# Second-stage weights split once, half of them kept and half reloaded; ScalarE shares the counting in every routing phase

## The chip, the cores and the metric

One core of one Trainium2 chip runs the whole program. The metric is the device time of an execution in microseconds (us). The core's engines work side by side, each through its own fixed list of instructions in order: TensorE (PE, matrix products, with its weight loads shown as PEld), VectorE (DVE), ScalarE (ACT), GpSimd (POOL), and SyncE (SP), which here only issues transfers (DMAs). An engine that has to wait for another stands still, and everything behind the waiting instruction in its list stands with it.

## The reference

```
x = attention(q, k, v, M_prev, z_prev, beta)      # 4 batches x 576 tokens = 2304 tokens, 512 wide
logits = x @ w_gate                               # 8 experts
order = argsort(-logits.flatten())                # greedy: best pair of token and expert first
# a token is given to the first expert in that order that has fewer than cap = 288 tokens
for e in range(8):
    h = maximum(x[mask_e] @ w1[e], 0)             # 512 -> 1024
    out[mask_e] = h @ w2[e]                       # 1024 -> 512
# second layer, the same for all tokens
h = out @ w_in                                    # 512 -> 2048, float64 in the inputs
g = h * clip(h + 3, 0, 6) / 6
return g @ w_out                                  # 2048 -> 512, float64 in the inputs
```

Results are wanted at float32 precision, so the kernel writes each float32 operand of a product as the sum of a rounded part (hi) and what is left (lo), and makes three products: hi hi, hi lo, lo hi.

## The kernel before

**Two stages.** First comes the attention with the gate's logits. While it runs, class `Convert` turns w_in and w_out from float64 into float32, 28 of 32 pieces (`PRE`), and stores them in a DRAM tensor `wb`. Then comes `experts`: eight turns of one loop, numbered s = 0 to 7 here and below. Turn s takes the 288 tokens of the expert that fills up as number s, through that expert's own weights (kind 0, 8 blocks f of 128 hidden units) and then through the shared second layer (kind 1, 16 blocks f). A step of the loop is one block: `l1` (12 products of 128x128 by 288 columns into `h`), an activation that leaves `gh` and `gl`, and two steps later (`LAG`) `l2` (12 products into four accumulators).

**The weights.** The shared layer's weights lie in one float32 tile `WB`, 16 blocks of 128x1024. `split_w` makes hi and lo of each half block afresh for every step of all eight turns: ScalarE copies the 512 columns to `wh`, and GpSimd subtracts to get `wl`, with every sixth subtraction on VectorE (`EVERY`). `ahead` runs this up to three steps (`SPLIT`) before the products. An expert's own weights come by DMA into `raw` (four buffers) and are split in the same way. The last 4 of the 32 float64 pieces are converted in the first two steps of turn 0 (`rest`), into `WB`; the other 28 are loaded from `wb` in seven transfers of 1 MB.

**The routing.** `Router.phase(s)` finds which expert fills up as number s and with which tokens. It is a chain, run on VectorE for the most part, cut into units by `yield`; `step()` works them into turn s - 1 at a fixed rate per step (`RATE`). From phase 2 on, keys go out to DRAM and come back spread over all partitions (`kd<-ks`, `rHw<-kd`, `rLw<-kd`, issued by SP). Two searches follow (`search`), of four rounds each. A round compares all 2304 16-bit values with a threshold T per partition and counts them (L714), turns the counts round (L723) and picks the next T (L726), so a round starts from the result of the one before. In phase 0 alone, which runs at the end of the attention, ScalarE counts 864 of the values with a Sign (L717), and one small instruction (L718) adds its count. The routing for s = 7 is trivial, so turns 6 and 7 have no search, and turn 5 has only the end of a phase.

**What sets the order.** The code's order gives the dependences; a scheduler then fixes each engine's list at build time. On SP too, a transfer whose buffer is not yet free holds up those behind it.

Of the kernel before, what the change touches and what calls it, by code (L numbers as in the profile page):

```python
# [28 lines left out]
SHARE = 432  # L29
# [485 lines left out]
class Router:  # L515
# [188 lines left out]

    def search(self, W, need, row, shared):


        nc, wk = self.nc, self.wk
        T = self.T0
        W, cmp = [x.rearrange("p b s -> p (b s)") for x in (W, self.cmp)]  # L710
        n = W.shape[1] - shared
        for s in range(4):
            cnt = wk.tile([128, 1], F32, name="cnt", bufs=2)
            nc.vector.tensor_scalar(cmp[:, :n], W[:, :n], T, 0.0, op0=OP.is_ge, op1=OP.add, accum_out=cnt)  # L714
            if shared:
                below = wk.tile([128, 1], F32, name="below", bufs=2)
                nc.scalar.activation(cmp[:, n:].bitcast(BF), W[:, n:], AF.Sign, bias=T, scale=-1.0, accum_out=below)  # L717
                nc.vector.scalar_tensor_tensor(cnt, below, -0.5, cnt, op0=OP.mult, op1=OP.add)  # L718
            if s == 0:
                yield 0  # L720
            else:
                nc.vector.tensor_scalar(self.G[:, s, 32:], T, self.cz[:, s:s + 1], None, op0=OP.add)
            nc.vector.transpose(row[:, s, :32], cnt.to_broadcast([128, 32]))  # L723
            fl = wk.tile([128, 33], F32, name="fl", bufs=2)
            T = wk.tile([128, 1], F32, name="T", bufs=4)
            nc.vector.scalar_tensor_tensor(fl, row[:, s], need, self.G[:, s], op0=OP.is_ge, op1=OP.mult, accum_out=T)  # L726
            yield SLACK
        self.found = T
# [76 lines left out]
    def phase(self, s):  # L805
# [6 lines left out]
        if s < E - 1:  # L812
# [10 lines left out]
            else:  # L823
                self.by_dram()
                yield BACK
            half = SHARE if s == 0 else 0
            Hs = self.search(self.Hw, cap - half, self.rowH, 2 * half)
# [11 lines left out]
            c = self.rowH[:, :, :32]  # L839
            if half:  # L840
                nc.vector.tensor_scalar(m, c, float(half), None, op0=OP.add)
                c = m
            nc.vector.scalar_tensor_tensor(m, c, cap, c, op0=OP.is_lt, op1=OP.mult)
# [109 lines left out]
class Convert:  # L953
# [51 lines left out]

    def rest(self, WB):

        for i in range(self.pre, len(self.src)):
            w = WB[:, i // 2, i % 2 * 512:(i % 2 + 1) * 512].rearrange("p (k n) -> p k n", k=4)
            self.load(i)  # L1010
            self.bits(w.bitcast(I32), i)
            self.sign(w, w, i)
            yield i // 2


def experts(ctx, tc, rt, x_dram, cv, w1, w2, out, ident, cap, B, S):
# [9 lines left out]
    NEXT = 12, 11  # L1026
    CONV = 2, 8
    EARLY = 6
    res = ctx.enter_context(tc.tile_pool(name="eres", bufs=1))
# [3 lines left out]
    rt.late(ctx, ps)  # L1033
    WB = res.tile([128, FB, 1024], F32, name="WB")

# [32 lines left out]

    def load_expert(s, f):
        if f == 0:  # L1070
# [5 lines left out]
        nc.sync.dma_start(raw[:, 512:], w2[bass.ds(e, 1), f * 128:(f + 1) * 128, :].rearrange("o p n -> p (o n)"))  # L1076
        raws[s, f] = raw

    W = {}
    cnt = [0]  # L1080

    def split_w(i, part):
        s, kind, f = order[i]
        src = (WB[:, f, :] if kind else raws[s, f])[:, part * 512:(part + 1) * 512]
        hi, lo = [wp.tile([128, 512], F32R, name=f"w{z}{part}", tag=f"w{z}{part}", bufs=SPLIT[part]) for z in "hl"]
        cnt[0] += 1
        nc.scalar.activation(hi, src, AF.Copy)  # L1087
        v = cnt[0] % EVERY == 0 or cnt[0] <= FIRST
        j = (nc.vector if v else nc.gpsimd).tensor_tensor(lo, src, hi.bitcast(F32), op=OP.subtract)  # L1089
        if s == 0 and kind == 0:  # L1090
            after(tc, j, rt.last if v else rt.fetch)
        W[i, part] = hi, lo
        if part and kind == 0 and f + RAW < FA:
            load_expert(s, f + RAW)

# [105 lines left out]
    def ahead(i):  # L1201

        for part, n in ((0, SPLIT[0]), (1, SPLIT[1] - LAG)):
            while nw[part] < min(i + n, len(order)):
                split_w(nw[part], part)
# [69 lines left out]
def body(ctx, tc, q, k, v, M_prev, z_prev, beta, w_gate, w1, w2, w_in, w_out, out, dbg=None):  # L1275
# [71 lines left out]
```

## Time and profile before

| | us |
|---|---|
| median of 3 runs | 1165.59 (1163.01 to 1169.36) |
| profiled execution: time / its span | 1169.76 / 1168.0 |
| attention and routing phase 0 | up to 346 |
| turns 0 to 7 of `experts` | 125.1, 112.0, 108.0, 108.8, 106.7, 93.0, 83.5, 75.0 |

A turn is counted here from the end of the turn before to the copies of its own result out of the accumulators (`yo`, L1130), read from the trace, to half a microsecond. Busy times are sums of the durations of an engine's instructions. TensorE's busy time is not its speed: successive 288-column products start 0.13 us apart at the full clock and 0.24 us apart at half of it, while each is shown some 0.3 to 0.6 us long, since they overlap. What TensorE waited for, and the clock it was granted, say more.

### The profile page before, as it was taken

The numbers are of one execution on the slowest core, as the hardware profiler recorded it, in microseconds if no ns is written. First come the engines' busy times: TensorE is split into PE (matmuls) and PEld (weight loads), VectorE is DVE, ScalarE is ACT, GpSimd is POOL, SyncE is SP. The second block draws the span as 40 slices with busy tenths as digits, with TensorE's granted clock in tenths as the row PEclk, the third lists the DMA queues.
The fourth block names the chain that finished last, engine by engine and source line by source line (L and its number), as shares of the span: only waits on it lengthen the run. The fifth ranks groups of instructions, "written<-read, shape, count | busy, mean of one in ns | idle before, by whom it ended". The sixth has DMA issues, their size and how long they took to land.

```text
span 1168.0 us, 20128 instructions
## 1 busy us (share of the span) xinstructions
PE 984.3 (84%) x6748; PEld 903.9 (77%) x6748; DVE 854.6 (73%) x1935; ACT 673.2 (58%) x1627; POOL 664.1 (57%) x514
## 2 busy tenths in 40 slices
PE   4988898897228797898899798879978999999997
PEld 3666776675128697888798788779978999999996
DVE  7788887886867987868866976897497755455453
ACT  5776876774326354445545463555545567667674
POOL 7666666461436364654565465547544567767773
PEclk9999998898559888889999898899898899999999
DMA  7888878875344023121132023104201400401100
GB/s 173 241 232 250 241 191 254 225 202 162 149 150 194 1 87 86 61 92 41 55 112 64 1 80 107 44 1 134 81 16 39 127 22 19 147 21 37 57 2 21
DMA packets 103560, 123.17 MB, mean 105 GB/s; under 512 B 19744, under 2 KB 70304, under 8 KB 102560
## 3 DMA queue, kind: packets, MB, share of 16 engines
q1 hardware_dynamic: 99120, 108.22, 32.1%
q0 software_dynamic: 3072, 9.44, 2.7%
q10 hardware_dynamic: 1264, 4.22, 0.9%
q8 instruction: 53, 0.87, 0.3%
q14 instruction: 51, 0.42, 0.1%
HBM read 85.88 MB, written 17.22 MB: 88 GB/s over the span
## 4 chain that ended last, share of the span: by engine, by line
PE 41%; DVE 35%; DMA 12%; issue 7%; ACT 3%; SPq 2%; POOL 1%; POOLq 0%; DVEq 0%; ACTq 0%
DVE rcmp L714 9%; PE acc L1099 5%; PE acc L1100 5%; PE h L1170 5%; PE h L1167 5%; PE acc L1098 5%; PE h L1168 5%; DMA rHw<-kd 3%; DVE gl L1188 3%; PE av L328 3%; PE rp L701 3%; DVE t L1186 2%; DVE wl L1089 1%; DMA raw<-in_moe_w_in_dram 1%; DVE fl L726 1%
## 5 line engine op out<-in xcount | busy, mean ns | idle before, releaser
L1089 POOL TENSOR_TENSOR wl<-WB,wh 128x512 fp32r<-128x512 f32 x215 | 290.6, 1367 | 216.9 <-ACT wh L1087 198.2
L1099 PE MATMUL acc<-gl,wh 128*128 128x288 f32 x768 | 237.8, 318 | 54.4 <-DVE gl L1188 48.2
L1100 PE MATMUL acc<-gh,wl 128*128 128x288 f32 x768 | 232.1, 311 | 0.0
L1099 PEld LDWEIGHTS acc<-gl,wh 128*128 128x128 f32 x768 | 156.1, 203 | 62.7 <-DVE gl L1188 55.6
L1098 PE MATMUL acc<-gh,wh 128*128 128x288 f32 x768 | 196.9, 312 | 8.6 <-ACT gh L1187 8.6
L1087 ACT ACTIVATE wh<-WB 128x512 fp32r<-128x512 f32 x256 | 159.3, 631 | 39.5 <-PE acc L1099 35.8
L1089 POOL TENSOR_TENSOR wl<-raw,wh 128x512 fp32r<-128x512 f32 x100 | 134.4, 1357 | 66.5 <-ACT wh L1087 61.8
L1100 PEld LDWEIGHTS acc<-gh,wl 128*128 128x128 f32 x768 | 156.2, 203 | 0.0
L1167 PE MATMUL h<-yh,wh 128*128 128x288 f32 x512 | 147.1, 308 | 1.3 <-ACT pc L1185 1.3
L1098 PEld LDWEIGHTS acc<-gh,wh 128*128 128x128 f32 x768 | 138.2, 200 | 10.5 <-ACT gh L1187 10.1
L1168 PE MATMUL h<-yh,wl 128*128 128x288 f32 x512 | 145.3, 304 | 0.0
L1188 DVE SCALAR_TENSOR_TENSOR gl<-t,gh 128x288 fp32r<-128x288 f32 x128 | 104.3, 823 | 35.9 <-ACT gh L1187 35.8
L1186 DVE SCALAR_TENSOR_TENSOR t<-t,pc 128x288 f32<-128x288 f32 x128 | 75.8, 594 | 63.4 <-ACT pc L1185 63.3
L1184 ACT ACTIVATE t<-h,rthree 128x288 f32<-128x288 f32 x128 | 63.7, 497 | 98.3 <-PE h L1170 75.6
L1187 ACT ACTIVATE gh<-t 128x288 fp32r<-128x288 f32 x128 | 56.3, 443 | 100.7 <-DVE t L1186 100.6
L1167 PEld LDWEIGHTS h<-yh,wh 128*128 128x128 f32 x512 | 101.4, 198 | 3.5 <-ACT pc L1185 2.8
L282 ACT ACTIVATE P<-P,mx 128x128 f32<-128x128 f32 (+2 forms) x144 | 83.7, 583 | 34.6 <-DVE mx L267 33.1
L1168 PEld LDWEIGHTS h<-yh,wl 128*128 128x128 f32 x512 | 101.3, 198 | 0.3 <-POOL wl L1089 0.2
L1170 PE MATMUL h<-yl,wh 128*128 128x288 f32 x512 | 96.4, 309 | 5.6 <-DVE yl L1158 5.6
L1087 ACT ACTIVATE wh<-raw 128x512 fp32r<-128x512 f32 x128 | 81.6, 640 | 21.3 <-issue 10.4
L1170 PEld LDWEIGHTS h<-yl,wh 128*128 128x128 f32 x512 | 79.6, 198 | 7.6 <-DVE yl L1158 7.0
L1181 DVE TENSOR_TENSOR gl<-t,gh 128x288 fp32r<-128x288 f32 x64 | 51.3, 801 | 38.4 <-ACT gh L1180 38.2
(283 smaller groups left out, 2360.6 us busy)
## 6 DMA issues: line engine op xcount, KB each, us to landing
raw<-in_moe_w_dram SPq DMA_DIRECT2D x128, 256.0 KB
kh<-knh SPq DMA_DIRECT2D x60, 144.0 KB
raw<-in_moe_w_in_dram SPq DMA_DIRECT2D x16, 512.0 KB
raw<-in_moe_w_out_dram SPq DMA_DIRECT2D x16, 512.0 KB
wb<-wf SPq DMA_DIRECT2D x28, 256.0 KB
kn<-in_k_dram SPq DMA_DIRECT2D x16, 288.0 KB
qn<-in_q_dram SPq DMA_DIRECT2D x16, 288.0 KB
qs<-qnh SPq DMA_DIRECT2D x30, 144.0 KB
```

What stands on the lines that cost most here:

```text
L282: nc.scalar.activation(x[:, :w], x[:, :w], AF.Exp, bias=mx, scale=-1.0, accum_out=col)
L714: nc.vector.tensor_scalar(cmp[:, :n], W[:, :n], T, 0.0, op0=OP.is_ge, op1=OP.add, accum_out=cnt)
L1087: nc.scalar.activation(hi, src, AF.Copy)
L1089: j = (nc.vector if v else nc.gpsimd).tensor_tensor(lo, src, hi.bitcast(F32), op=OP.subtract)
L1098: nc.tensor.matmul(p, ah, bh, start=first, stop=False)
L1099: nc.tensor.matmul(p, ah, bl, start=False, stop=False)
L1100: rt.behind = nc.tensor.matmul(p, al, bh, start=False, stop=last)
L1167: nc.tensor.matmul(p, wk[k][0], x[k][0], start=(k == 0), stop=False)
L1168: nc.tensor.matmul(p, wk[k][1], x[k][0], start=False, stop=False)
L1170: rt.behind = nc.tensor.matmul(p, wk[k][0], x[k][1], start=False, stop=(k == KC - 1))
L1186: nc.vector.scalar_tensor_tensor(t, t, 6.0, pc, op0=OP.min, op1=OP.mult)
L1188: nc.vector.scalar_tensor_tensor(gl, t, 1.0 / 6.0, gh.bitcast(F32), op0=OP.mult, op1=OP.subtract)
```

## The change

`split_w` now splits the shared weights only in turn 0. Odd blocks f get their hi and lo written into `WB`, which has become a tile of 8 blocks x 2 halves x (512 hi + 512 lo), as many bytes as before, and they stay there. Even blocks are split into a rotating tile `w0` or `w1`, written to a new DRAM tensor `hl` by SP, and in turns 1 to 7 read back, 16 transfers of 512 KB a turn. In turn 0 the float32 blocks come through the `raw` buffers, one transfer each; the four unconverted pieces are converted when their block's turn in `load` comes (`conv`), one per step. In turns 1 to 7 all remaining subtractions (kind 0) are GpSimd's. `ahead` runs as far as the rotating tiles allow, up to six steps. And the sharing of the count with ScalarE holds in all phases.

```diff
@@ search
-            if shared:
-                below = wk.tile([128, 1], F32, name="below", bufs=2)
-                nc.scalar.activation(cmp[:, n:].bitcast(BF), W[:, n:], AF.Sign, bias=T, scale=-1.0, accum_out=below)
-                nc.vector.scalar_tensor_tensor(cnt, below, -0.5, cnt, op0=OP.mult, op1=OP.add)
+            below = wk.tile([128, 1], F32, name="below", bufs=2)
+            nc.scalar.activation(cmp[:, n:].bitcast(BF), W[:, n:], AF.Sign, bias=T, scale=-1.0, accum_out=below)
+            nc.vector.scalar_tensor_tensor(cnt, below, -0.5, cnt, op0=OP.mult, op1=OP.add)
@@ phase
-            half = SHARE if s == 0 else 0
+            half = SHARE
-            if half:
-                nc.vector.tensor_scalar(m, c, float(half), None, op0=OP.add)
-                c = m
+            nc.vector.tensor_scalar(m, c, float(half), None, op0=OP.add)
+            c = m
@@ experts
-    WB = res.tile([128, FB, 1024], F32, name="WB")
+    WB = res.tile([128, FB // 2, 2, 1024], F32R, name="WB")
+    hl = cv.dram.tile([FB // 2, 2, 128, 1024], F32, name="hl")
+    def load(s, j):
+        if j >= FA + FB * (s == 0):
+            return
+        if j >= FA:
+            f = j - FA
+            raw = raws[s, 1, f] = wp.tile([128, 1024], F32, name="raw", tag="raw", bufs=RAW)
+            if f < cv.pre // 2:
+                nc.sync.dma_start(raw, cv.wb[:, f])
+            else:
+                conv.extend([lambda u=u: cv.rest(raw[:, u * 512:(u + 1) * 512], 2 * f + u) for u in range(2)])
+            return
...
@@ split_w
-        src = (WB[:, f, :] if kind else raws[s, f])[:, part * 512:(part + 1) * 512]
-        hi, lo = [wp.tile([128, 512], F32R, name=f"w{z}{part}", tag=f"w{z}{part}", bufs=SPLIT[part]) for z in "hl"]
+        if kind and f % 2:
+            w = WB[:, f // 2, part]
+        else:
+            w = wp.tile([128, 1024], F32R, name=f"w{part}", tag=f"w{part}", bufs=SPLIT[part])
+        hi, lo = w[:, :512], w[:, 512:]
+        W[i, part] = hi, lo
+        if kind and s:
+            if f % 2 == 0:
+                nc.sync.dma_start(w.bitcast(F32), hl[f // 2, part])
+            return
+        src = raws[s, kind, f][:, part * 512:(part + 1) * 512]
         cnt[0] += 1
         nc.scalar.activation(hi, src, AF.Copy)
-        v = cnt[0] % EVERY == 0 or cnt[0] <= FIRST
+        v = s == 0 and (cnt[0] % EVERY == 0 or cnt[0] <= FIRST)
         j = (nc.vector if v else nc.gpsimd).tensor_tensor(lo, src, hi.bitcast(F32), op=OP.subtract)
...
+        if kind and f % 2 == 0:
+            nc.sync.dma_start(hl[f // 2, part], w.bitcast(F32))
+        if part:
+            load(s, f + kind * FA + RAW)
@@ ahead
-        for part, n in ((0, SPLIT[0]), (1, SPLIT[1] - LAG)):
-            while nw[part] < min(i + n, len(order)):
+        for part in range(2):
+            while nw[part] < min(i + 2 * SPLIT[0], len(order)):
+                held = [j for j in range(i - part * LAG, nw[part] + 1) if j >= 0 and not (order[j][1] and order[j][2] % 2)]
+                if len(held) > SPLIT[part] or order[nw[part]][0] not in reg or order[nw[part]][:1] + (0, 0) not in raws:
+                    break
                 split_w(nw[part], part)
                 nw[part] += 1
@@ before and in the loop
-    for f in range(0, EARLY, 2):
-        nc.sync.dma_start(WB[:, f:f + 2], cv.wb[:, f:f + 2])
-    rest = cv.rest(WB)
+    for i in range(2):
+        cv.load(cv.pre + i)
...
-        if s == 0 and f % FA < CONV[1]:
-            for _ in range(CONV[0]):
-                next(rest, None)
+        if conv:
+            conv.pop(0)()
```

Two places show what this does to the engines' lists. The first is ScalarE's list in turn 3, at the searches of phase 4; `t`, `pc` and `gh` are the three activations of a step of kind 1, `wh0` and `wh1` the hi copies of a half block. Before:

```order
L1184 ACTIVATE t_7653<-h_7626,rthree_181 128x288
L1185 ACTIVATE pc_7654<-h_7626 128x288
L1087 ACTIVATE wh0_7660<-WB_4127 128x512
L1087 ACTIVATE wh1_7664<-WB_4127 128x512
L1187 ACTIVATE gh_7651<-t_7653 128x288
```

In the changed kernel, at the same place (`rcmp, below` is the Sign with its count, `T` the threshold that VectorE found in the round before):

```order
L1204 ACTIVATE t_7591<-h_7555,rthree_181 128x288
L1205 ACTIVATE pc_7592<-h_7555 128x288
L716 ACTIVATE rcmp_178,below_7634<-rHw_176,T_7575 128x864
L1207 ACTIVATE gh_7589<-t_7591 128x288
L716 ACTIVATE rcmp_178,below_7695<-rHw_176,T_7640 128x864
L1204 ACTIVATE t_7625<-h_7598,rthree_181 128x288
L1205 ACTIVATE pc_7626<-h_7598 128x288
```

The two copies of each step are gone, and a Sign stands in their place, sometimes ahead of the next step's `t` and sometimes behind its `pc`.

The second place is SP's list around the keys of phase 4. Before, the way out and the two ways back stand together:

```order
L1076 DMA raw_7957<-in_moe_w2_dram 128x512
L759 DMA kd_7541<-ks_7540 64x576
L762 DMA rHw_176<-kd_7541 128x1x2304
L762 DMA rLw_177<-kd_7541 128x1x2304
L1074 ISA
L1074 DMA raw_8189<-in_moe_w1_dram 128x4x128
```

In the changed kernel the reads of `hl` stand ahead of them and between them:

```order
L1102 DMA w1_7428<-hl_4128 128x1024
L1102 DMA w0_7395<-hl_4128 128x1024
L1102 DMA w0_7479<-hl_4128 128x1024
L758 DMA kd_7444<-ks_7443 64x576
L1102 DMA w1_7481<-hl_4128 128x1024
L761 DMA rHw_176<-kd_7444 128x1x2304
L761 DMA rLw_177<-kd_7444 128x1x2304
L1102 DMA w0_7551<-hl_4128 128x1024
```

One read of `hl` has moved between the way out and the first way back, and the two before the way out wait for buffers that the products of earlier steps set free.

## Rows read from the trace of the kernel before

**Rows 1.** Stretches by turn, 0 to 7: busy us (instructions), granted clock, DMA share, GB/s.

```profile
346.40:471.50 125.10, 105.68 (x661) 99.89 (x662) 101.23 (x198) 64.41 (x147) 64.04 (x48) 0.86 0.28 93
471.50:583.50 112.00, 96.25 (x654) 91.56 (x653) 91.85 (x180) 57.43 (x135) 60.84 (x46) 0.92 0.21 63
583.50:691.50 108.00, 95.27 (x636) 92.14 (x635) 82.05 (x153) 56.52 (x134) 59.34 (x46) 0.91 0.22 64
691.50:800.30 108.80, 91.27 (x635) 87.91 (x634) 85.29 (x154) 55.77 (x133) 60.01 (x46) 0.92 0.20 62
800.30:907.00 106.70, 93.38 (x633) 90.17 (x633) 80.14 (x154) 56.52 (x132) 58.76 (x46) 0.90 0.21 63
907.00:1000.00 93.00, 90.58 (x651) 89.71 (x650) 57.83 (x111) 56.00 (x130) 59.81 (x46) 0.94 0.19 59
1000.00:1083.50 83.50, 81.10 (x602) 80.22 (x601) 43.28 (x62) 56.05 (x129) 59.11 (x46) 0.98 0.21 66
1083.50:1158.50 75.00, 74.64 (x566) 74.10 (x564) 36.97 (x55) 49.44 (x112) 48.54 (x37) 1.00 0.05 16
```

The engines in each row are PE, PEld, DVE, ACT and POOL, in that order.

**Rows 2.** Page of the profile: the chain's shares by engine, and ScalarE's copies of WB.

```profile
PE 41%; DVE 35%; DMA 12%; issue 7%; ACT 3%; SPq 2%; POOL 1%; POOLq 0%; DVEq 0%; ACTq 0%
...
L1087 ACT ACTIVATE wh<-WB 128x512 fp32r<-128x512 f32 x256 | 159.3, 631 | 39.5 <-PE acc L1099 35.8
```

**Rows 3.** Waits in the whole span: total us, times, longest us.

```profile
ACT gh L1187 <- DVE t L1186: 100.6, 46, 5.0
...
PE acc L1099 <- DVE gl L1188: 48.2, 32, 4.4
...
DVE rcmp L714 <- DMA rHw<-kd: 18.9, 6, 5.0
```

**Rows 4.** VectorE by line in 691 to 800 us: busy us, mean ns, idle before.

```profile
L1188 DVE SCALAR_TENSOR_TENSOR gl<-t,gh 128x288 fp32r<-128x288 f32 x16 | 15.3, 966 | 0.4 <-ACT gh L1187 0.4
L1186 DVE SCALAR_TENSOR_TENSOR t<-t,pc 128x288 f32<-128x288 f32 x16 | 9.5, 594 | 5.9 <-ACT pc L1185 5.9
L714 DVE TENSOR_SCALAR_CACHE_REDUCE rcmp<-rLw,T 128x2304 uint16<-128x2304 uint16 x3 | 7.8, 2611 | 0.1
...
L1089 DVE TENSOR_TENSOR wl<-WB,wh 128x512 fp32r<-128x512 f32 x5 | 4.6, 924 | 0.0
...
L1089 DVE TENSOR_TENSOR wl<-raw,wh 128x512 fp32r<-128x512 f32 x3 | 2.0, 681 | 0.0
```

**Rows 5.** Tile rcmp: ns min/median/max, first and last start, forms.

```profile
L714 DVE TENSOR_SCALAR_CACHE_REDUCE rcmp<-rHw,T x21: 1711/2611/2615, 301.2 to 859.5; 128x2304 uint16<-128x2304 uint16 x18, 128x1440 uint16<-128x1440 uint16 x3
...
L717 ACT ACTIVATE rcmp<-rHw,T x3: 1014/1014/1016, 301.2 to 309.1; 128x864 bf16<-128x864 uint16 x3
L717 ACT ACTIVATION_READ_ACCUMULATOR rcmp<-rHw,T x3: 186/186/187, 302.1 to 310.0; 128x1 f32 x3
```

**Rows 6.** Line 718, the added count, in phase 0: ns min/median/max.

```profile
L718 DVE SCALAR_TENSOR_TENSOR cnt<-below,cnt x8: 142/160/1534, 298.9 to 325.5; 128x1 f32<-128x1 f32 x8
```

**Rows 7.** Line 1188 in the whole span: ns min/median/max.

```profile
L1188 DVE SCALAR_TENSOR_TENSOR gl<-t,gh x128: 414/608/2064, 399.6 to 1155.2; 128x288 fp32r<-128x288 f32 x128
```

**Rows 8.** VectorE, then GpSimd, in order of time around 748 us: start us, length us.

```profile
748.67 1.51 DVE L1188 SCALAR_TENSOR_TENSOR gl<-t,gh 128x288 fp32r<-128x288 f32 x1
...
745.71 4.16 POOL L1089 TENSOR_TENSOR wl<-WB,wh 128x512 fp32r<-128x512 f32 x3 [6.57 <-ACT wh L1087]
```

**Rows 9.** Chain that ended last, from 815 us: start us, length us, what.

```profile
840.27 6.85 DMA rHw<-kd
```

**Rows 10.** Stretch in which loads of 1 MB from wb run (columns as in rows 1).

```profile
313.00:316.00 3.00, 0.00 (x0) 0.00 (x0) 3.00 (x6) 0.00 (x0) 0.63 (x1) 0.50 1.00 410
```

**Rows 11.** GpSimd, then TensorE, in order of time from 337 us, at turn 0's start.

```profile
337.12 5.26 POOL L1064 DMA_INDIRECT xg<-x_dram,ids  x1 [23.49 <-DVE rleft L916]
...
344.55 0.92 POOL L1064 DMA_INDIRECT xg<-x_dram,ids  x1 [0.30 <-issue]
...
346.38 2.41 PE L1113 MATMUL xt<-ident,xg 96*128 96x96 f32 x12 [10.15 <-DMA xg<-x_dram,ids]
```

More of the change, by code (lines that the diff above doesn't have):

```diff
@@ L1004, in run, with rest @@
                                    f.rearrange("p k n -> p (k n)").bitcast(F32))
[L1006 to L1013, printed above, removed]
+    def rest(self, w, i):
+        w = w.rearrange("p (k n) -> p k n", k=4)
+        self.bits(w.bitcast(I32), i)
+        self.sign(w, w, i)
+        if i + 2 < len(self.src):
+            self.load(i + 2)
 def experts(ctx, tc, rt, x_dram, cv, w1, w2, out, ident, cap, B, S):
@@ L1026, in experts @@
     NEXT = 12, 11
-    CONV = 2, 8
-    EARLY = 6
     res = ctx.enter_context(tc.tile_pool(name="eres", bufs=1))
@@ L1067, in gather @@
             rt.fetch = i
-    def load_expert(s, f):
+    def load(s, j):
[9 more added lines that the diff above has]
+            return
+        f = j
         if f == 0:
@@ L1076, in load_expert @@
         nc.sync.dma_start(raw[:, 512:], w2[bass.ds(e, 1), f * 128:(f + 1) * 128, :].rearrange("o p n -> p (o n)"))
-        raws[s, f] = raw
+        raws[s, 0, f] = raw
     W = {}
+    conv = []
     cnt = [0]
@@ L1091, in split_w @@
             after(tc, j, rt.last if v else rt.fetch)
-        W[i, part] = hi, lo
-        if part and kind == 0 and f + RAW < FA:
-            load_expert(s, f + RAW)
+        if kind and f % 2 == 0:
+            nc.sync.dma_start(hl[f // 2, part], w.bitcast(F32))
+        if part:
+            load(s, f + kind * FA + RAW)
     def mm3(p, lhs, rhs, first, last):
@@ L1225, in experts @@
     for f in range(RAW):
-        load_expert(0, f)
-    for f in range(0, EARLY, 2):
-        nc.sync.dma_start(WB[:, f:f + 2], cv.wb[:, f:f + 2])
-    rest = cv.rest(WB)
+        load(0, f)
+    for i in range(2):
+        cv.load(cv.pre + i)
     cv.behind = rt.last
@@ L1232, in experts @@
         pass
-    for f in range(EARLY, cv.pre // 2, 2):
-        i = nc.scalar.dma_start(WB[:, f:f + 2], cv.wb[:, f:f + 2])
-        after(tc, i, rt.xin)
     def step():
@@ L1246, in experts @@
             for u in range(RAW):
-                load_expert(s + 1, u)
+                load(s + 1, u)
             xs = x_in(s + 1)
@@ L1293, in body @@
     cv = Convert(ctx, tc, w_in, w_out, wb, PRE)
+    cv.dram = dram
     with ExitStack() as actx:
```

## The prediction

> **What bounds the kernel now.** I read the stretches by turn first [rows 1]. Turn 7, without any routing, takes 75.0 us at a granted clock of 1.00, with TensorE busy throughout: that is what 24 steps cost TensorE. Turn 6, with the tail of a phase but no search, takes 83.5 us. Turns 1 to 4, with searches, take 106.7 to 112.0 us at a clock of 0.90 to 0.92. So some 25 us of each of these four turns come with the routing, though its products are few. What differs between the rows is VectorE: busy for 37.0 us in turn 7, 43.3 in turn 6, 57.8 in turn 5, and 80.1 to 91.9 in turns 1 to 4. Next the chain that ended last: VectorE has 35% of it, ScalarE 3%, GpSimd 1% [rows 2]. Then the waits [rows 3]: TensorE's largest is for `gl`, 48.2 us in 32 waits; ScalarE waits 100.6 us for VectorE's `t` before it can make `gh`; and VectorE itself stands 18.9 us at the first comparison of six phases, because the keys have not come back. VectorE's list is in order, so a `gl` behind a comparison waits for it. GpSimd and ScalarE are busy for little over half of a turn [rows 1], so work taken off them counts only by what it does to VectorE.
>
> **The change, part by part.** All sums are for the profiled execution, 1169.76 us. I work them out in turn 3 (85.3 us of VectorE) and carry them to the others.
>
> *Counting.* A comparison of 2304 values takes 2.61 us, one of 1440 takes 1.71 [rows 5]. Eight rounds a phase give 8 x 0.90 = 7.2 us less. Each round gains the added count, 0.160 us by its median in phase 0 [rows 6], and the phase gains one small addition to `m`, which I count as a ninth of these: 1.4 us more. ScalarE's Sign takes 1.01 + 0.19 = 1.20 us [rows 5], less than the 1.71 beside it, so it is hidden when it starts within half a microsecond of the comparison. What it costs when it does not is a rival below.
>
> *Splitting, on VectorE.* In turns 1 to 7 VectorE no longer subtracts: in turn 3 that takes away 4.6 + 2.0 = 6.6 us [rows 4].
>
> *Splitting, on GpSimd.* 32 subtractions of kind 1 a turn go, and with them a collision. In turn 3 `gl` takes 966 ns and `t` 594 on average [rows 4], while the shortest `gl` takes 414 [rows 7]. One `gl` took 1.51 us beside a row of three GpSimd subtractions of 1.39 us each [rows 8]. Without them I take 450 ns for both, near the shortest: 16 x 0.516 + 16 x 0.144 = 10.6 us. The bounds are 0 (if the lengthening is VectorE's own) and 16 x 0.552 + 16 x 0.180 = 11.7.
>
> The Trainium skill has a rule for this (SBUF — State Buffer, section "SBUF: two separate sides"): GpSimd and a VectorE instruction with two SBUF inputs share one port pair under an exclusive lock, and whichever comes second waits out the whole of the first. By that rule all of the lengthening goes where GpSimd falls silent, so the sum would stand at 10.6. It also speaks against the change in one place: in kind 0 of turns 1 to 7 GpSimd now does all 16 subtractions, so `gl` there stays long.
>
> *Splitting, on ScalarE.* 32 copies of 631 ns a turn go [rows 2], 20 us, and 8 Signs come, 9.6 us. I count nothing for it: ScalarE stood mostly waiting for VectorE [rows 3]. That gain has a bound of its own in the first rival.
>
> VectorE's 85.3 us in turn 3 so become 85.3 - 7.2 + 1.4 - 6.6 - 10.6 = 62.3. For what that is worth I go by the rows of turns 4 and 5: between 80.1 us busy (106.7 us long) and 57.8 (93.0) a microsecond of VectorE is worth 13.7 / 22.3 = 0.61 of the turn [rows 1]. This slope has the waits and the lost clock in it. With the same 23.0 us off, turn 1 becomes 99.7 us (12.3 less), turn 2 93.8 (14.2), turn 3 95.7 (13.1), turn 4 92.6 (14.1). Turn 5 has no rounds left (the last comparison of the keys starts at 859.5 us [rows 5], in turn 4), keeps the end of a phase, and loses 17 us of VectorE; it cannot fall below turn 6, and I take 86 (7 less). Turn 6 gives 1.5, turn 7 nothing. Sum: 62.2.
>
> *Turn 0.* The splits stay. The shorter rounds give 5.8 x 0.61 = 3.5. At its start TensorE waits 10.15 us for the gather, whose first list took GpSimd 5.26 us to write and its third 0.92, while VectorE was converting two pieces [rows 11]; these now come in mid-turn. The most this can give is 4.3; I take 3. Sum with the turns: 68.7.
>
> *Reloading.* 16 reads of 512 KB a turn, 8.4 MB. From `wb`, of the same form, the transfers reached 410 GB/s with every DMA engine busy [rows 10], so the reads take 20 us of a turn of 94, where the DMA share is 0.2 now [rows 1]. A buffer is free some five steps before its next use, 15 us, so TensorE should not wait for them. The place where they can hurt is the way back of the keys, 6.85 us [rows 9], for which VectorE already waits. One read now stands between the way out and the way back: 0.52 MB at 410 GB/s is 1.3 us, in five phases 6.4. The bounds are 0 (the buffer is free and the read done before the keys have reached DRAM) and, for a read that waits for a step of TensorE (75 / 24 = 3.1 us) besides, 5 x 4.4 = 22. I take 6.4, so 68.7 - 6.4 = 62.3 is left. In turn 0 the new writes and the loads through `raw` move 16 MB in 118 us, under half of that rate; nothing for them.
>
> 1169.76 - 62.3 = 1107.5 us. The median of the runs is 4.2 under the profiled execution, so 1103 is forecast.
>
> **The rivals.**
>
> *TensorE's bound is reached.* VectorE's relief and ScalarE's together end the waits, and turns 1 to 4 come to 86.5 us, turn 6 plus the few products of keys and turning. For it: TensorE's waits in these turns are nearly all for VectorE. Against: the wait for the keys stays. Gain 25.5 + 21.5 + 22.3 + 20.2 = 89.5, turn 5 8, turn 0 10, turn 6 1.5: 109, so 1057. Chance 0.18.
>
> *`gl` stays long.* If the lengthening isn't GpSimd's, VectorE keeps 10.6 us a turn: 10.6 x 0.61 = 6.5 in four turns, and 4 in turn 5: 30 less gain, 1133. Against it speaks the row of 1.51 us [rows 8]. Chance 0.10.
>
> *The reads come late.* The keys' way back is held 4.4 us in each of five phases, and TensorE waits for a read now and then: 16 to 28 us less gain, about 1125. Chance 0.08.
>
> *Slower: VectorE and ScalarE in lockstep.* A Sign can start only when ScalarE gets to it. In the new list it stands behind `t` and `pc` of a step whose products may not be done, or ahead of them, holding them until VectorE has a threshold. VectorE's added count waits for the Sign, behind it `gl` and the next round, and TensorE behind `gl`. There are 48 such rounds in the turns, and each can lose up to a step, 3.1 us. From 62.3 / 48 = 1.3 us a round beyond the cover it eats the gain; at 2 us it costs 96, so 1103 + 96 = 1199. For it: ScalarE's longest wait for VectorE's `t` is 5.0 us [rows 3], so the two are already bound to each other. Against: `l2` runs two steps behind `l1`, about 6 us of slack, and VectorE's own `t` of the same step waits for the same products anyway. Chance 0.09.
>
> *Nothing.* TensorE's clock falls as its work gets denser and gives the gain back: 1165. Turns 6 and 7, the densest, have the highest clock [rows 1]. Chance 0.04.
>
> **How the numbers follow.** 0.51 is left for the forecast, 1080 to 1125 by its own bounds (`gl` and `t` at their shortest and half of ScalarE's relief, against the late keys). With the reads' and `gl`'s rivals above it and the nearer half of the first rival below, the range is 1050 to 1150; outside are the lockstep, no change, and the far end of the first. About 0.5% is what a measurement can tell from no change: faster by more than that 0.87, within it 0.04, slower 0.09.
>
> **What would show it.** In the profile after: 1440-value comparisons of 1.71 us in all phases, no `wl` on VectorE after turn 0, `gl` of kind 1 near 450 ns from turn 1 on, VectorE busy for about 60 to 70 us in turns 1 to 4, these turns at 92 to 100 us with a clock above 0.93, and TensorE's waits for `gl` well under half of 48 us. The forecast is wrong if VectorE's waits for the Sign add up to more than a few microseconds a phase, if TensorE waits for `hl` at all, or if the keys' way back takes 10 us or more.

## The result: 1132.8 us, faster by 2.8%, half of the gain forecast

The changed kernel takes 1132.76 us in the median of 4 runs (1130.45 to 1136.23), beside 1167.47 for the kernel before on the same chip: a ratio of 0.9717, 95% interval 0.9686 to 0.9748. The forecast was 1103. The profiled execution took 1130.45 us, its span is 1128.6. One of the four runs of the experiment e2 below, 1158.73 us, fell into the chip's slower state and is left out of its median and ratio.

First the stretches by turn of the kernel after, 0 to 7, in the columns of [rows 1]:

```profile
341.60:472.10 130.50, 106.07 (x672) 98.81 (x673) 98.03 (x207) 76.18 (x171) 64.60 (x48) 0.85 0.56 181
472.10:571.20 99.10, 89.11 (x629) 85.27 (x628) 72.31 (x193) 51.80 (x123) 28.68 (x22) 0.97 0.49 153
571.20:673.90 102.70, 91.27 (x651) 88.26 (x650) 63.96 (x155) 49.54 (x119) 27.28 (x23) 0.97 0.50 147
673.90:772.90 99.00, 91.14 (x634) 88.55 (x633) 61.51 (x154) 47.68 (x116) 26.75 (x23) 0.93 0.51 153
772.90:872.00 99.10, 90.53 (x635) 87.07 (x634) 62.58 (x155) 48.22 (x116) 26.65 (x23) 0.95 0.49 153
872.00:964.80 92.80, 90.54 (x651) 90.21 (x650) 40.07 (x102) 39.45 (x98) 27.37 (x23) 0.94 0.46 150
964.80:1044.10 79.30, 78.94 (x602) 78.68 (x602) 28.22 (x53) 39.15 (x97) 26.88 (x23) 1.00 0.53 175
1044.10:1119.10 75.00, 74.64 (x567) 74.23 (x565) 23.00 (x46) 31.84 (x78) 13.83 (x12) 1.00 0.39 128
```

The first number after each stretch is its length. VectorE's busy time (third engine) fell as worked out in turn 3, 85.3 to 61.5 us, where 62.3 was forecast; in turns 1, 2 and 4 it fell by 19.5, 18.1 and 17.6 us, where 23.0 had been carried over from turn 3. The lengths did not follow everywhere. Turn 5 lost 18 us of VectorE and is as long as it was; turn 0 grew by 5 us. TensorE (first engine) is now busy for over 90 us of the 99 in turns 3 and 4.

VectorE's rows in turn 3 after, by line (columns as in [rows 4]):

```profile
L1208 DVE SCALAR_TENSOR_TENSOR gl<-t,gh 128x288 fp32r<-128x288 f32 x16 | 7.9, 498 | 1.6 <-ACT gh L1207 0.9 <-PE acc L1120 0.5
L1206 DVE SCALAR_TENSOR_TENSOR t<-t,pc 128x288 f32<-128x288 f32 x16 | 7.3, 453 | 9.6 <-ACT pc L1205 9.6
L714 DVE TENSOR_SCALAR_CACHE_REDUCE rcmp<-rLw,T 128x1440 uint16<-128x1440 uint16 x3 | 5.1, 1711 | 0.1
```

`gl` of kind 1 fell from 966 to 498 ns and `t` from 594 to 453 [rows 4], a comparison takes 1711 ns, and no `wl` is left. Then waits of the whole span (answering [rows 3]), and the page's shares of the chain:

```profile
DVE t L1206 <- ACT pc L1205: 117.2, 79, 3.8
ACT gh L1207 <- DVE t L1206: 64.4, 74, 4.7
ACT rcmp L716 <- DVE fl L725: 41.0, 35, 4.1
DVE rcmp L714 <- DMA rHw<-kd: 31.7, 6, 8.2
ACT rcmp L716 <- DMA rHw<-kd: 30.7, 5, 8.7
PE acc L1119 <- DVE gl L1208: 15.6, 18, 2.3
PE acc L1118 <- ACT gh L1207: 14.5, 11, 4.3
DVE cnt L717 <- ACT rcmp L716: 1.2, 1, 1.2
```

```profile
PE 34%; DVE 20%; issue 8%; DMA 5%; ACT 1%; POOL 1%; POOLq 0%; DVEq 0%; ACTq 0%; SPq 0%
```

TensorE's wait for `gl` went from 48.2 to 15.6 us. The chain's shares cannot be set beside [rows 2]: this chain starts at 338.6 us, so they add up to 69% of the span. Of the eight turns alone, VectorE's pieces of the chain are 38% before and 29% after. VectorE hardly ever waits for a Sign (1.2 us, all of it in phase 0). But its stand for the keys grew from 18.9 to 31.7 us. ScalarE, which now needs the keys too, stands 30.7 us with them and 41.0 us for thresholds of VectorE's (`fl`, L725; 10.5 before, all in phase 0), and VectorE waits 117.2 us for ScalarE's `pc` (63.3 before). Most of the longer stand for the keys is not the reads' doing: it is 26.8 us in e9 and 26.1 in e10 below, neither of which reloads anything.

The turns of the main kernels, from the same view of each trace (start of turn 0, then lengths; in us). Each row is one execution, up to 8 us from its kernel's median (e1: 1164.64 beside 1172.31). A part of the routing's products can fall into turn 1 or into turn 2 (TensorE has 651 instructions in turn 2 after, 633 in e10), so these two are best read together:

| | start | 0 | 1 | 2 | 3 | 4 | 5 | 6 | 7 |
|---|---|---|---|---|---|---|---|---|---|
| before | 346.4 | 125.1 | 112.0 | 108.0 | 108.8 | 106.7 | 93.0 | 83.5 | 75.0 |
| after | 341.6 | 130.5 | 99.1 | 102.7 | 99.0 | 99.1 | 92.8 | 79.3 | 75.0 |
| e1_count_only | 339.0 | 130.5 | 116.3 | 105.4 | 107.5 | 105.4 | 92.1 | 82.2 | 75.0 |
| e2_weights_only | 341.1 | 135.9 | 108.6 | 100.3 | 100.4 | 100.7 | 92.8 | 79.4 | 75.1 |
| e5_convert_early | 346.3 | 123.5 | 105.1 | 100.1 | 100.0 | 98.1 | 92.6 | 79.3 | 75.1 |
| e6_compare_twice | 344.4 | 145.2 | 116.6 | 105.3 | 107.1 | 102.5 | 93.9 | 79.3 | 75.1 |
| e7_gpsimd_busy | 342.2 | 140.8 | 113.8 | 116.1 | 107.3 | 106.5 | 96.8 | 79.7 | 75.0 |
| e9_no_subtractions | 341.8 | 125.6 | 100.4 | 99.2 | 97.7 | 99.1 | 91.4 | 79.3 | 74.8 |
| e10_no_reads | 340.5 | 132.4 | 108.0 | 93.2 | 96.0 | 96.3 | 94.0 | 79.3 | 75.1 |
| e11_early_and_back10 | 345.6 | 122.4 | 100.1 | 102.4 | 100.1 | 102.8 | 87.9 | 79.3 | 75.1 |

### The profile page after: what moved, and what is told of

Its sections match the earlier page's. It is cut to its first block, busy times and chain, and to the rows that moved or that the text cites. A ratio compares the mean times of both kernels' runs of the same rounds, so it can differ in the third digit from the quotient of the medians.

```text
span 1128.6 us, 20123 instructions
## 1 busy us (share of the span) xinstructions
PE 961.0 (85%) x6748; PEld 885.6 (78%) x6748; DVE 727.9 (64%) x1933; ACT 605.6 (54%) x1499; POOL 435.8 (39%) x346
## 4 chain that ended last, share of the span: by engine, by line
PE 34%; DVE 20%; issue 8%; DMA 5%; ACT 1%; POOL 1%; POOLq 0%; DVEq 0%; ACTq 0%; SPq 0%
DVE rcmp L714 5%; PE h L1187 5%; PE acc L1119 5%; PE h L1188 5%; PE acc L1120 5%; PE h L1190 5%; PE acc L1118 5%; DMA rHw<-kd 4%; PE rp L701 2%; DVE gl L1201 2%; DVE gl L1208 2%; DVE cnt L717 1%; DVE t L1206 1%; DVE fl L725 1%; POOL w L1108 1%
## 5 line engine op out<-in xcount | busy, mean ns | idle before, releaser
L1108 POOL TENSOR_TENSOR w<-raw,w 128x512 fp32r<-128x512 f32 x135 | 180.6, 1352 | 383.5 <-ACT w L1106 291.4
L1119 PE MATMUL acc<-gl,w 128*128 128x288 f32 x512 | 156.7, 312 | 19.3 <-DVE gl L1208 13.0
L1120 PE MATMUL acc<-gh,w 128*128 128x288 f32 x512 | 153.4, 306 | 0.0
L1118 PE MATMUL acc<-gh,w 128*128 128x288 f32 x512 | 139.9, 310 | 13.7 <-ACT gh L1207 13.5
L1206 DVE SCALAR_TENSOR_TENSOR t<-t,pc 128x288 f32<-128x288 f32 x128 | 61.4, 480 | 117.4 <-ACT pc L1205 117.2
L1119 PEld LDWEIGHTS acc<-gl,w 128*128 128x128 f32 x512 | 101.8, 199 | 24.3 <-DVE gl L1208 16.7
L1204 ACT ACTIVATE t<-h,rthree 128x288 f32<-128x288 f32 x128 | 63.5, 496 | 102.8 <-PE h L1190 97.5
L1118 PEld LDWEIGHTS acc<-gh,w 128*128 128x128 f32 x512 | 93.9, 197 | 16.3 <-ACT gh L1207 16.2
L1106 ACT ACTIVATE w<-raw 128x512 fp32r<-128x512 f32 x144 | 89.6, 633 | 28.5 <-PE acc L1120 16.3
L1120 PEld LDWEIGHTS acc<-gh,w 128*128 128x128 f32 x512 | 101.8, 199 | 0.0
L1208 DVE SCALAR_TENSOR_TENSOR gl<-t,gh 128x288 fp32r<-128x288 f32 x128 | 66.1, 517 | 29.8 <-ACT gh L1207 28.0
L1187 PE MATMUL h<-yh,w 128*128 128x288 f32 x256 | 74.4, 309 | 6.6 <-ACT pc L1205 6.6
L1119 PE MATMUL acc<-gl,WB 128*128 128x288 f32 x256 | 75.9, 303 | 2.7 <-DVE gl L1208 2.6
L1187 PE MATMUL h<-xh,w 128*128 128x288 f32 x256 | 75.3, 313 | 0.3 <-ACT gh L1200 0.3
L1120 PE MATMUL acc<-gh,WB 128*128 128x288 f32 x256 | 74.8, 298 | 0.0
L1188 PE MATMUL h<-xh,w 128*128 128x288 f32 x256 | 74.4, 310 | 0.0
L1188 PE MATMUL h<-yh,w 128*128 128x288 f32 x256 | 72.5, 301 | 0.0
```

The lines of the kernel that those rows point to most:

```text
L1118: nc.tensor.matmul(p, ah, bh, start=first, stop=False)
L1119: nc.tensor.matmul(p, ah, bl, start=False, stop=False)
L1120: rt.behind = nc.tensor.matmul(p, al, bh, start=False, stop=last)
L1187: nc.tensor.matmul(p, wk[k][0], x[k][0], start=(k == 0), stop=False)
L1188: nc.tensor.matmul(p, wk[k][1], x[k][0], start=False, stop=False)
L1204: nc.scalar.activation(t, p, AF.Relu, bias=rt.three)
```

## The experiments

Times are medians; ratios are to the kernel before, run on the same chip beside each, with their 95% intervals. The experiments ran on several chips, so differences from the changed kernel ("after") are worked out from the two ratios and 1167 us.

**One part alone: the counting.** The kernel before, with one line changed:

```
-            half = SHARE if s == 0 else 0
+            half = SHARE
```

> The kernel before with the shared count in all phases and nothing else. Theory K (after the change, what holds turns 1 to 4 is the return of the keys, at which VectorE and now ScalarE stand, and TensorE's own products; a microsecond of VectorE is worth less than 0.61): ScalarE still has its 32 copies of WB a turn here, so a Sign that waits for the keys holds these too; 5 to 15 us faster than before. Theory V (VectorE's busy time sets the turn at 0.61 us per us, as in the prediction): 7.2 - 1.4 = 5.8 us of VectorE a phase, six phases, 0.61: 21 us faster. Theory L (VectorE and ScalarE in lockstep): no gain or slower.

1172.31 us, 1.0058 (1.0040 to 1.0077): slightly slower. In the table turns 2 to 4 are 1 to 3 us shorter, turns 0 and 1 are 5 and 4 longer. Taking comparisons off VectorE by itself brings nothing, and the reason is that VectorE got no relief: it is busy for 441.8 us in turns 0 to 4, 440.6 before. The comparisons take 43 us less, but the 48 added counts take 0.75 us each, where 0.16 had been priced, and `fl` goes from 14.5 to 26.6 us. VectorE's counts in turns 0 to 4, then one of them from VectorE's list and what GpSimd does beside it:

```profile
L718 DVE SCALAR_TENSOR_TENSOR cnt<-below,cnt 128x1 f32<-128x1 f32 x48 | 35.9, 749 | 0.1
```

```profile
768.04 1.24 DVE L718 SCALAR_TENSOR_TENSOR cnt<-below,cnt 128x1 f32<-128x1 f32 x1
767.76 1.51 POOL L1089 TENSOR_TENSOR wl<-WB,wh 128x512 fp32r<-128x512 f32 x1 [2.19 <-ACT wh L1087]
```

The count ends 0.01 us after the subtraction, and so it is with all 25 counts of over 0.3 us: each ends within 0.03 us after the end of a subtraction of GpSimd's, while its Sign had been done 0.9 us or more before it began.

**The other part alone: the weights.** The changed kernel with counting shared in phase 0 only:

```
-            half = SHARE
+            half = SHARE if s == 0 else 0
```

> The changed kernel with the shared count in phase 0 alone, as before the change. K: VectorE gets 5.8 us a phase back, but ScalarE no longer stands at the keys, so t and pc go on while VectorE stands: 1130 to 1142 us, 0 to 10 slower than the changed kernel. V: six phases x 5.8 x 0.61 = 21 us slower than the changed kernel, 1154. L: faster than the changed kernel by 10 us or more.

1145.59 us, 0.9823 (0.9751 to 0.9895), 12 more than after, give or take 9. So sharing costs 7 us where the shared weights are still split in every turn and brings some 12 where they aren't. The two traces differ by 15.1 us; the table has nearly all of it in turns 0 and 1 (5.4 and 9.5 us), nothing in turns 2 to 4.

**More time for the keys.** The first round comes four units of the routing's chain later, some two steps of the loop:

```
-BACK = 6
+BACK = 10
```

> The changed kernel with the pause between the sending of the keys and the first comparison set to 10 instead of 6, some two steps of TensorE more. K: the first comparison stands 3 us or less for the keys instead of 4 to 8, in five phases: 10 to 25 us faster than the changed kernel, 1108 to 1123. V: VectorE has the same work, so within 5 us of 1133. L: the same, since the rounds themselves are unchanged.

1137.64 us, 0.9735 (0.9691 to 0.9780). No gain: VectorE's stand at the keys only fell from 31.7 to 28.7 us. Turn 5 fell to 85.2 us, the others gave that back.

**First round on VectorE alone**, in phases 1 to 6, so that no Sign stands in front of `t` while the keys are away:

```
+            k = W.shape[1] if alone and s == 0 else n
+            nc.vector.tensor_scalar(cmp[:, :k], W[:, :k], T, 0.0, op0=OP.is_ge, op1=OP.add, accum_out=cnt)
+            if k > n:
+                nc.vector.tensor_scalar(cnt, cnt, -0.5 * shared, None, op0=OP.add)
```

> The changed kernel, but the first round of the search in the high halves is counted by VectorE alone in phases 1 to 6, so no Sign waits for the keys in ScalarE's list. VectorE gets 0.9 us more a phase. K: ScalarE's t and pc go on while VectorE stands at the keys, 1 to 3 us a phase: 5 to 15 us faster than the changed kernel. V: 6 x 0.9 x 0.61 = 3 us slower. L: 0 to 3 us faster, one Sign in eight gone.

1137.69 us, 0.9751 (0.9708 to 0.9795): no gain. Turns 3 and 4 fall by 1.7 and 1.1 us, turn 1 rises by 10.6. Over turns 2 to 4 TensorE's waits for ScalarE's `gh` and `pc` do fall, from 13.5 to 5.9 us, and the turns by 3.2 us in all; ScalarE's 30.7 us with the keys are worth no more than that.

**The conversions back to the start of turn 0.** All 32 pieces go through `wb`, and the last four are converted in turn 0's first two steps, where they were before the change:

```
-PRE = 28
+PRE = 32
+        if i > 28 and self.behind is None:
+            return
-    conv = []
+    conv = [cv.run] * 4
```

> The changed kernel with the last four float64 pieces converted in the first two steps of turn 0, as before the change (through wb). Theory C: in mid-turn they cost VectorE 10.8 us among the search's rounds, while at the start VectorE stands for the gather anyway; turn 0 goes from 130 to 120 to 125 us, 5 to 10 faster than the changed kernel. Rival W: turn 0 grew by the writes to hl, the loads through raw and the Signs beside 32 copies; then within 3 us of the changed kernel, or slower by up to 4, since the gather's list is written beside the conversions.

1129.71 us, 0.9688 (0.9620 to 0.9755). Turn 0 falls by 7 us to 123.5, but it starts 4.7 later; the total is not resolved from that of the changed kernel.

**Every comparison twice**, in phases 1 to 6, the second unused:

```
+            if again:
+                c2 = wk.tile([128, 1], F32, name="c2", bufs=2)
+                nc.vector.tensor_scalar(cmp[:, :n], W[:, :n], T, 0.0, op0=OP.is_ge, op1=OP.add, accum_out=c2)
```

> The changed kernel with VectorE's 1440-value comparison made twice in each round of phases 1 to 6, the second count unused: 8 x 1.8 = 14.3 us of VectorE more a phase. Theory V (0.61 of a turn per us of VectorE, as predicted): 6 x 14.3 x 0.61 = 52 us slower than the changed kernel. Theory K2 (VectorE is no longer what turns 1 to 4 wait for in the main; TensorE's own products, its clock and short waits make up what is left): below 25 us slower, most of it in turns 0 and 1, where VectorE is fullest.

1180.95 us, 1.0101 (1.0045 to 1.0158), 45 more than after: near Theory V's 52 and far from Theory K2's "below 25". So added work on VectorE still costs: in turns 0 and 1 VectorE is 35.3 us busier and they are 32.2 longer; in turns 2 to 4 it is 29.5 us busier and they are 14.1 longer, 0.48 each. Over turns 1 to 4 it is 0.62 each.

**GpSimd busy again.** 32 unused subtractions of 128x512 a turn where the old ones stood, turns 1 to 7:

```
+            d = rt.R.rearrange("p d b n -> p (d b n)").bitcast(F32)
+            nc.gpsimd.tensor_tensor(d, d, d, op=OP.subtract)
```

> The changed kernel with 32 subtractions of 128x512 on a dead tile put on GpSimd in kind 1 of turns 1 to 7, in place of those that are gone; nobody waits for them. If GpSimd's subtractions are what lengthened gl and t: gl of kind 1 in turn 3 from 498 to 700 ns or more, t from 453 to 550 or more, and the turns with a search longer by 2 to 6 us each, 10 to 30 us in all by V's slope, 5 to 12 by K2; turns 6 and 7 unchanged. If not: gl below 550 and within 3 us of the changed kernel.

1188.22 us, 1.0179 (1.0120 to 1.0239): 54 more than after, slower than before even. VectorE's rows in its turn 3, by line:

```profile
L1210 DVE SCALAR_TENSOR_TENSOR gl<-t,gh 128x288 fp32r<-128x288 f32 x16 | 15.1, 954 | 1.0 <-ACT gh L1209 1.0
L1208 DVE SCALAR_TENSOR_TENSOR t<-t,pc 128x288 f32<-128x288 f32 x16 | 13.8, 867 | 2.8 <-ACT pc L1207 2.5
```

`gl` is back at 954 ns (966 before, 498 after) and `t` at 867, with nothing changed on VectorE but its neighbour. The subtractions, themselves hardly on the path that sets the end (GpSimd has 1% of the chain, and TensorE never waits for it), are what made VectorE long. From the page, over the whole span:

```profile
L1102 POOL TENSOR_TENSOR rR<-rR 128x512 f32<-128x512 f32 x224 | 249.0, 1111 | 13.8 <-PE rw L701 2.7
L1208 DVE SCALAR_TENSOR_TENSOR t<-t,pc 128x288 f32<-128x288 f32 x128 | 100.7, 789 | 84.1 <-ACT pc L1207 83.6
L1210 DVE SCALAR_TENSOR_TENSOR gl<-t,gh 128x288 fp32r<-128x288 f32 x128 | 91.4, 718 | 28.7 <-ACT gh L1209 27.8
```

In the changed kernel the same 128 `t` and 128 `gl` take 61.4 and 66.1 us: 65 us less of VectorE. Instructions of the routing are longer too: in all VectorE is busy for 846.2 us, 727.9 after, 118 us more.

**The keys on a queue of their own.** kd, rHw and rLw of phases 2 to 6 go out on GpSimd's queue, past the reads:

```
-            nc.sync.dma_start(W.rearrange("p b s -> p (b s)"), bass.AP(
+            q.dma_start(W.rearrange("p b s -> p (b s)"), bass.AP(
```

> The changed kernel with the keys' way out and back (kd, rHw, rLw of phases 2 to 6) issued by GpSimd on its own queue, so that no read of hl stands between them or ahead of them. If the reads hold them up: the way back at 7 us again instead of 8 to 10, VectorE's wait there from 31.7 to 20 us or less. K (this stall costs TensorE): 5 to 15 us faster than the changed kernel. K2 (two steps of slack hide most of it): within 4 us.

1147.36 us, 0.9818 (0.9768 to 0.9869), 12 more than after. The ways back on the chain that ended last (start us, us), and one row of GpSimd's list:

```profile
534.30 7.65 DMA rHw<-kd
630.41 10.53 DMA rHw<-kd
729.75 10.42 DMA rHw<-kd
827.33 14.78 DMA rHw<-kd
```

```profile
627.95 0.57 POOL L759 DMA_DIRECT2D kd<-ks  x1 [9.13 <-ACT ks L757]
```

Three of the four ways back take 10.42 to 14.78 us (6.85 to 7.23 before, 8.55 to 10.15 after), so a queue without reads on it did not bring the 7 us back. Whether the reads still hold them up there or the other queue is slower of itself is not shown: no run sends the keys by it without the reads. And GpSimd now stands 9.13 us at the issue of `kd`, until ScalarE has made `ks`, with its own subtractions queued behind. Which of these costs the 12 us was not taken apart.

**The subtractions taken away alone.** The kernel before without the lower parts of the shared weights in turns 1 to 7; the products use the upper part twice, so that TensorE's work is the same. Every sixth of these had been VectorE's own. Copies and counting stay as they were, nothing is reloaded:

```
+        if s and kind:
+            W[i, part] = hi, lo
+            return
         v = cnt[0] % EVERY == 0 or cnt[0] <= FIRST
```

> The kernel before, with the lower parts of the shared weights left out in turns 1 to 7 (224 subtractions fewer on GpSimd and VectorE; the products take the upper part twice, so TensorE's work is unchanged). Theory V (GpSimd's subtractions were the dear part of the old second stage, and the new kernel pays some of that gain out again in turn 0 and on the keys' way back): this kernel reloads nothing and counts in halves in phase 0 only, and gains as much as the whole change or more: turns 1 to 4 at 98 to 102 us, gl of kind 1 near 500 ns, the keys' way back 7 us as before, turn 0 unchanged at 125 to 127 us; 1110 to 1130 us. Rival S (the subtractions hurt only where counting and copies are there too; the gain needs all the parts together): VectorE still counts alone and ScalarE still copies, turns 1 to 4 stay at 104 to 107 us; 1140 to 1155 us.

1122.95 us, 0.9641 (0.9600 to 0.9681): 42 us, more than the 33 of the whole change. Its turn 3, and VectorE's waiting for the keys over the whole span:

```profile
667.00:764.70 97.70, 89.47 (x634) 87.14 (x634) 68.40 (x149) 55.58 (x132) 23.25 (x19) 0.95 0.23 69
```

```profile
DVE rcmp L714 <- DMA rHw<-kd: 26.8, 6, 6.0
```

VectorE counts all 2304 values here and is 6.9 us busier than in the changed kernel; the turn is 1.3 us shorter all the same.

**No reads.** The changed kernel, where an even block's products in turns 1 to 7 take the resident block beside it:

```
-        if kind and f % 2:
+        if kind and (s or f % 2):
-            if f % 2 == 0:
-                nc.sync.dma_start(w.bitcast(F32), hl[f // 2, part])
```

> The changed kernel without the 112 reads of stored weights (each even block's products take the resident block beside it; everything else stays). Theory R (the reads lengthen the keys' way back, and that wait ends turns 1 to 5): the way back falls from 8 to 10 us to about 7, DVE's stand at the keys from 31.7 us to under 24, turns 1 to 5 lose 1.5 to 3 us each; 1118 to 1125 us. Rival H (the transfers lie in time that nobody waits for; VectorE's own list and the start of each turn set the end): 1130 to 1136 us, whatever the way back shows.

1128.82 us, 0.9673 (0.9641 to 0.9704), between the two theories and not resolved from after. From the chains that ended last, the way back in turns 2 to 4, first after, then here:

```profile
615.45 9.99 DMA rHw<-kd
714.06 8.55 DMA rHw<-kd
812.43 10.15 DMA rHw<-kd
```

```profile
620.89 7.26 DMA rHw<-kd
714.39 7.40 DMA rHw<-kd
810.88 7.12 DMA rHw<-kd
```

The reads lengthen it by 2.3 us a phase (9.56 less 7.26 in the mean), and without them turns 2 to 4 are 9.5, 3.0 and 2.8 us shorter. Turn 1, at a clock of 0.91 in place of 0.97, gave 8.9 back; turns 1 to 4 together are 6.4 us shorter.

**The two edits that shortened a turn, together:** that of e5 and `BACK = 10`.

> The changed kernel with the last four conversions done in the first two steps of turn 0 and with BACK 10 in place of 6, the two edits that each shortened one turn (turn 0 from 130.5 to 123.5 us, turn 5 from 92.8 to 85.2 us) while others grew. If the turns add up one by one: 1130 less 7 less 7, 1114 to 1120 us. If what one turn saves comes back in its neighbours, since the lists only shift against each other: 1128 to 1136 us.

1126.48 us in the median of 6 (1118.82 to 1127.36), 0.9631 (0.9600 to 0.9661). This interval lies below that of the changed kernel: of the versions that compute all of the result this is the fastest, 10 us under the changed kernel by the ratios and 6 by the medians. The turns did not simply add up (turn 4 is 3.7 us longer than after).

## Why the prediction was half right

**VectorE's sum held in turn 3, and not when it was carried over.** Rounds, subtractions and the collision with GpSimd came to 62.3 us in turn 3, measured 61.5. The Trainium skill's rule (SBUF — State Buffer, section "SBUF: two separate sides"), by which GpSimd and a VectorE instruction with two SBUF inputs shut each other out, agrees with the trace: `gl` at 498 ns without the subtractions, 954 with them. Its warning for kind 0 came true as well: `gl` there takes 824 ns in the mean, 801 before. But turn 3 had the longest `gl` of all turns, and two terms do not hold elsewhere. VectorE's rows of kind 1's `gl` in turn 4 before, and of the added counts in turns 0 to 4 after:

```profile
L1188 DVE SCALAR_TENSOR_TENSOR gl<-t,gh 128x288 fp32r<-128x288 f32 x16 | 10.0, 641 | 0.1
```

```profile
L717 DVE SCALAR_TENSOR_TENSOR cnt<-below,cnt 128x1 f32<-128x1 f32 x48 | 19.6, 409 | 0.7 <-DVE cnt L844 0.3
```

In turn 4 there was little to win back at `gl` (641 ns to 499). And an added count was priced at 0.160 us, its median in phase 0; it takes 0.41, and 0.75 in e1, since it waits out GpSimd's subtractions like `gl`. So turns 1 to 4 lost 79.0 us of VectorE and not 4 x 23.0 = 92.

The subtractions and the collision were 4.6 + 10.6 = 15.2 of turn 3's 23.0 us as far as e9 takes them away (kind 0's stay in it), by the prediction's slope about 41 of the 62 us that turns 1 to 6 were to lose. e9 gained 42 (37 to 47, from its ratio). This term was right.

**The slope was the step that failed, for all that came beside the subtractions:** "between 80.1 us busy (106.7 us long) and 57.8 (93.0) a microsecond of VectorE is worth 13.7 / 22.3 = 0.61 of the turn". Its lower point was not VectorE's. In [rows 1] TensorE is busy 90.58 of turn 5's 93.00 us, and after the change, with 17.8 us less on VectorE, turn 5 takes 92.8, with 2.3 us of waits of TensorE. It was to lose 7 us and lost 0.2. (It is 85.2 us in e3 and 87.9 in e11, but there some 24 of TensorE's 651 instructions have moved to other turns.) For turns 1 to 4, these are VectorE's busy time and the length in seven kernels, sums over the four turns in us:

| | VectorE busy | length |
|---|---|---|
| before | 339.3 | 435.5 |
| e1_count_only | 339.8 | 434.6 |
| e6_compare_twice | 311.4 | 431.5 |
| e9_no_subtractions | 275.6 | 396.4 |
| e2_weights_only | 274.2 | 410.0 |
| after | 260.4 | 399.9 |
| e10_no_reads | 257.9 | 393.5 |

From before to e9 a microsecond of VectorE was worth 39.1 / 63.8 = 0.61, just as forecast. After has 15.2 us less of VectorE than e9 and is 3.5 us longer; without the reads (e10) 17.7 us less bring 2.9. And e2, as busy as e9, is 13.6 us longer. So VectorE's busy time alone does not set a turn: what went with the subtractions was paid at the full price, the rest of the change taken together was not.

TensorE's own rows say what stood in the way. In turns 2 to 4 after it is busy for 90.5 to 91.3 us (86.9 to 88.4 in e10). The forecast lengths, 92.6 to 95.7, left 2 to 5 us for its waits, little more than turn 5 has, where there is no search; they are 7.9 to 11.5. And they changed hands. TensorE's waits in turn 4, before and after:

```profile
PE acc L1099 <- DVE gl L1188: 10.6, 6, 2.9
PE acc L1099 <- DVE gl L1181: 2.0, 1, 2.0
```

```profile
PE h L1187 <- ACT pc L1205: 2.9, 1, 2.9
PE acc L1118 <- ACT gh L1207: 2.7, 2, 2.1
PE acc L1119 <- DVE gl L1208: 0.9, 2, 0.5
```

Over turns 2 to 4 its waits for `gl` fell from 31.3 to 8.5 us, those for ScalarE's `gh` and `pc` rose from 5.4 to 13.5. So little was left there that less work on VectorE could shorten. The counting brought nothing in turns 2 to 4; what it did bring, beside resident weights, lay in turns 0 and 1 (e2). What holds ScalarE up is open in part: it now stands at its Signs for keys and thresholds, and e4, which takes one Sign in eight away, got 7.6 of the 13.5 us back, but also counts more on VectorE.

Of the forecast's 62, turns 2 to 5 account for the larger part of the miss: they were to give 48 before the keys' way back, and gave 23.

**Turn 0 had the wrong sign.** Moving four conversions out of its start was to save 3 us there, since TensorE waits for the gather while VectorE converts [rows 11]. After, TensorE's wait is the same (GpSimd's, then TensorE's list in order of time):

```profile
332.41 4.95 POOL L1061 DMA_INDIRECT xg<-x_dram,ids  x1 [23.49 <-DVE rleft L914]
341.57 0.90 PE L1133 MATMUL xt<-ident,xg 96*128 96x96 f32 x4 [10.05 <-DMA xg<-x_dram,ids]
```

The first list takes 4.95 us (5.26 before), the wait 10.05 (10.15). The conversions had filled time in which VectorE had nothing else; in mid-turn they cost it 10.7 us, as VectorE's rows by line in turn 0 after add up:

```profile
L978 DVE TENSOR_SCALAR raw<-raw 128x512 int32<-128x512 int32 x4 | 3.5, 889 | 0.0
L981 DVE TENSOR_SCALAR raw<-raw 128x512 uint16<-128x512 int32 x4 | 2.8, 731 | 0.0
L979 DVE SCALAR_TENSOR_TENSOR raw<-raw 128x512 int32<-128x512 int32 x4 | 2.7, 684 | 0.0
...
L980 DVE TENSOR_SCALAR raw<-raw 128x512 int32<-128x512 int32 x4 | 1.7, 419 | 0.0
```

e5 puts them back and turn 0 becomes 7 us shorter. Turn 0 does start 4.8 us earlier, but so it does in e1 and e9, which move no conversion; over the kernels that start lies anywhere between 339.0 and 347.3, and why stays open.

**The reads.** 6.4 us were counted for the keys' way back. Turns 1 to 4 of e10 are 6.4 us shorter together, and its total is some 5 us lower (ratios 0.9717 and 0.9673, intervals overlapping), so the size was about right. The way back itself grew by 2.3 us a phase against e10, where 1.3 was counted, and once took 10.15 us: "10 us or more" was named as a sign of being wrong. That TensorE never waits for `hl` held.

**The rivals.** "TensorE's bound" was right in kind, not in size: its bound in turns 2 to 4 is nearer 90 us plus 8 to 12 of waits than 86.5. "`gl` stays long" gives 1133, the time measured, by a mechanism that the rows exclude. The lockstep did not come in the way described: VectorE waits 1.2 us for Signs, and in e1 the long counts wait for GpSimd, not for a Sign. That accounts for the gain that e1 lacks; where its 7 us go beyond that is not shown. Its other half, a Sign that holds up ScalarE's list until VectorE has a threshold, is in the rows, with 30.5 us of ScalarE's waits in turns 0 to 4. The granted clock did not simply follow the pauses. In turn 1 TensorE's waits fell from 15.8 to 9.8 us, and the stretch's mean of the two levels, 1.2 and 2.4 GHz, went from 0.92 to 0.97 of the upper; in turn 3 they fell more, from 17.5 to 7.9, and it went from 0.92 to 0.93.

**The account.** By the ratios the subtractions taken away alone (e9) bring 42 us, the whole change 33, and the change without the sharing (e2) 21: so the rest of the work on the weights takes some 21 us back, and sharing returns some 12. In the traces span before less after is 39.4 us, and e9 gives 49.2. The rest of the change takes 9.8 back, 4.9 of it in turn 0 and 6.2 in turns 2, 3 and 5, less 1.3 in turn 1, though it frees VectorE and ScalarE further. Turn 1 is the loosest of these numbers: in e5, which changes only what comes before it, it takes 105.1 us in place of 99.1, and 109.7 in e4.

## What to carry over

Before a slope is drawn between two stretches, look at the busy time of the other engines in both: where TensorE is busy for 90.6 of 93.0 us, that stretch is a floor and no point on VectorE's line. A slope that holds for one part of a change need not hold for the next: ask for each part which wait it shortens. Work that an idle-looking engine does can be the dearest part of a kernel through what it does to a neighbour; take it away alone first, since that may be worth more than the whole rebuild. A price read where a neighbour was quiet (0.16 us for the added count) is not the price beside a busy one (0.75). And ask of work moved out of a wait whether the wait was for it.

## What the runs showed of the hardware

The 224 subtractions of e7, 249 us of GpSimd's own time, added 118 us to VectorE's busy time, 65 of them in `t` and `gl` of kind 1, in instructions of which none was changed, and 54 us to the program. Size is no protection: a VectorE instruction of 128x1 with two inputs, 0.16 us long by itself, took 1.24 us when it met a subtraction, and ended 0.01 us after it (e1). And moving the keys' transfers to GpSimd's queue did not make them shorter (10.42 to 14.78 us in three of four in e8, 8.55 to 10.15 on SP's).
